# Soft-capped attention into a top-2 mixture of attention experts: the last two batches in packed passes of queries

## The chip, the cores and the metric

The kernel runs on one core of a Trainium2 chip. A core has five engines that run side by side and wait for each other through semaphores: TensorE (PE in the profile: matmuls and transposes into PSUM, with its weight loads as PEld), VectorE (DVE), ScalarE (ACT: tanh, exponentials, copies), GpSimd (POOL: casts, masks, the gate) and SyncE (SP: it issues DMA transfers). The metric is device microseconds of one execution. Three runs of the kernel before gave 313.25, 313.42 and 313.74 us, median 313.42.

## The reference

There are 8 batches, 12 heads, 448 positions and head size 64. The first stage is attention with a soft cap: scores are scaled by 1/8, passed through 30 tanh(s/30), and a softmax over the keys weighs v. The twelve heads of a position side by side are a row x of 768 numbers. The second stage is a mixture of four attention experts with a causal mask:

```python
scores = scale * np.matmul(q, k.transpose(0, 1, 3, 2))
scores = cap * np.tanh(scores / cap)
...
x = attn_out.transpose(0, 2, 1, 3).reshape(B, S, H * D)
logits = x @ w_gate
topk = np.argpartition(-logits, K, axis=-1)[..., :K]        # K = 2 of 4 experts
for e in range(E):
    q = x @ wq[e]; k = x @ wk[e]; v = x @ wv[e]
    scores = np.where(causal, -1000000000.0, scale * (q @ k.transpose(0, 2, 1)))
    a = softmax(scores)
    ye = a @ v @ wo[e]
    out += mask[..., None] * w[:, :, kk:kk + 1] * ye          # w: softmax over the two chosen logits
```

The softmax of either stage is made without its maximum: the exponentials are summed through a column of ones beside v, and the product is divided by that sum.

## The kernel before, in words

**First stage.** Two heads make a pair; there are 48 pairs, 6 a batch. A pair's q, k and v are loaded two pairs at a time (`load`), cast to 16 bits (`cast`, nearly all on POOL), and q and k are turned by TensorE and copied by VectorE into a tile `qk` (`tr`). Key rows are three chunks of 128 and a tail of 64. A step p then has three pieces: X (first key chunk of both heads, and the tails of both), Y1 and Y2 (second and third chunk). `fill` makes the scores into the PSUM tiles X (three banks) and Y (two banks), `tanh` runs on ScalarE over each piece, `expo` is one exponential over all seven rows of a step. `pv` multiplies with v, divides on VectorE (a reciprocal and a product) and `xt` turns the result into xT, from which the second stage of the batch reads. Three more PSUM banks, A0 to A2 (AUX), serve everything else.

**Steps.** In steps 0 to 41 (batches 0 to 6) a step is one pair with all its 448 queries. The pairs of batch 7 do their first 320 queries in steps 42 to 47; steps 48 and 49 do the last 128 queries of three pairs each. Thus there are 50 steps.

**Second stage.** For batches 0 to 5, `b_v`, `b_qk`, `b_gate` and `b_mask` project, choose and mask the queries by the chosen expert, and each of the two choices has one score block of 1024 columns (`b_score`) and its products (`b_pv`), sums (`b_ot`) and output (`b_wo`). For batch 6 (`FULL`), `e_score` and `e_pv` compute all four experts instead, in four blocks of 1024. Such a block takes the place of scores in X, and its exponential stands in ScalarE's list between those of the first stage. Batch 7's second stage (`last`, `last2`) runs after the first stage has ended: `last` for the first 320 queries, with a causal mask added in PSUM by a matmul (`negm`), and `last2` for the last 128.

**Order.** All instructions are recorded in a graph with costs (`Graph`, `Op`) and put in order by a list scheduler (`solve`) before they are issued. Each engine takes the most urgent ready instruction by its due time; the due times follow from ScalarE's fixed list of tanh and exponentials. `rank` adds a pseudo-random shift to the due time, drawn from `SEEDS`, one number for each 4 us of planned time. A `Group` holds one PSUM bank from its first matmul to its last reader. The order on each engine is fixed once built, and engines wait for one another at run time.

Of the kernel before, what the change touches and what calls it, by code (L numbers as in the profile page):

```python
# [8 lines left out]
f32 = mybir.dt.float32  # L9
# [13 lines left out]
SEEDS = (0, 0, 677, 116, 161, 0, 0, 56, 0, 513, 845, 569, 0, 188, 90, 308, 807, 654, 0, 873, 140, 943, 805, 400, 898, 250, 0, 621, 339, 0, 597, 460, 182, 0, 964, 592, 385, 0, 0, 0, 56, 980, 62, 160, 0, 0, 639, 563, 0, 0, 0, 105, 472, 832, 0, 567, 424, 0, 670, 583, 486, 783, 58, 224, 0, 0, 0, 0, 260, 212, 0, 946, 0, 0, 98, 0, 918, 79)  # L23
# [4 lines left out]
FDUE = 7.616  # L28
FULL = (6,)
XFULL = {5: (4, 5, 6, 7), 6: (4, 5, 6, 7)}  # L30
# [20 lines left out]
class Graph:  # L51
# [79 lines left out]
    def solve(self, when, banks, lent):  # L131
# [44 lines left out]
        while len(order) < n:  # L176
            best = None
            for e, rs in ready.items():
# [8 lines left out]
                def rank(x):  # L187
# [83 lines left out]
def kernel(  # L271
# [25 lines left out]
    PB = NP - HP  # L297
    W1 = 320
    NPV = NP + 2
    WIN1 = (0, 128, W1 - 128)  # L300
    TL = S - KM
    WIN = (0, 128, 256, S - 128)
    LB = B - 1

# [28 lines left out]
    PART = {"X": X[:, 0:2, :]}  # L333
# [66 lines left out]
    yp = [sb(f"yp{i}", [128, 7, S]) for i in range(NYP)]  # L400
    xk = [sb(f"xk{i}", [128, 4, 2, Dh]) for i in range(NXK)]
    rc2 = [sb(f"rc2_{i}", [128, 3, 2, 1], f32) for i in range(2)]
    xk2 = [sb(f"xk2_{i}", [128, 3, 2, Dh]) for i in range(2)]
    rca = [sb(f"rca{i}", [128, 2, 2, 1], f32) for i in range(4)]
# [3 lines left out]
    qB = [[sb(f"qB{i}_{r}", [128, S]) for r in range(2)] for i in range(2)]  # L408
    kB = [[sb(f"kB{i}_{r}", [128, S]) for r in range(2)] for i in range(2)]
# [6 lines left out]
    oT = [[sb(f"oT{i}_{r}", [128, S]) for r in range(2)] for i in range(2)]  # L416
# [12 lines left out]
    negm = sb("negm", [128, W1])  # L429
    neg2 = sb("neg2", [128, 2, 128])  # L430
    kL = sb("kL", [128, 2, 128])
    qL = sb("qL", [128, 2, 128])
    vL = sb("vL", [128, E, Dh + 1])
    p2 = yp[NPV % NYP].rearrange("p a s -> p (a s)")[:, 0 : E * 512].rearrange(
        "p (e c t) -> p e c t", e=E, c=4)
    oTL = [sb(f"oTL{i}", [128, 2, 128]) for i in range(2)]
    gt1 = [sb(f"gt1_{i}", sh, f32) for i, sh in enumerate(
        ([128, 3, E], [128, 3, E], [128, 3, E, E], [128, 2, 3, 1]))]
    gt2 = [sb(f"gt2_{i}", sh, f32) for i, sh in enumerate(
        ([128, 1, E], [128, 1, E], [128, 1, E, E], [128, 2, 1, 1]))]  # L440
# [89 lines left out]
    def setup_b():  # L530
# [25 lines left out]

        def lastc():
            nc.gpsimd.memset(vL[:, :, Dh : Dh + 1], 1.0)
            nc.gpsimd.memset(negm, 0.0)
            nc.gpsimd.memset(neg2, 0.0)  # L560
            nc.gpsimd.memset(neg2[64:128, 0, :], -30000.0)

        gp(0.9, lastc, w=["vL", "negm", "neg2"], due=150.0)

        def below(t, base):
            return lambda: nc.gpsimd.affine_select(
                out=t, in_=t, compare_op=ALU.is_ge, fill=-30000.0, base=base,
                pattern=[[1, 128]], channel_multiplier=-1)

        gp(0.4, below(negm[:, 0:128], 0), ["negm"], ["negm"], due=150.0)  # L570
        gp(0.4, below(negm[:, W1 - 128 : W1], -64), ["negm"], ["negm"], due=150.0)
        gp(0.4, below(neg2[:, 1, :], 0), ["neg2"], ["neg2"], due=150.0)
# [122 lines left out]
    def wid(p):  # L695
        return S if p < PB else W1 if p < NP else 3 * 128

    def of(p, what=None):


        if p < NP:
            return [p]
        ps = [PB + 3 * (p - NP) + i for i in range(3)]
        return ps if what is None else [ps[("X", "Y1", "Y2").index(what)]]

    def heads(p, what):
        dst = X if what == "X" else Y
        ci = {"X": 0, "Y1": 1, "Y2": 2}[what]
        t = qk[of(p, what)[0] % NQK]
        n = wid(p)  # L710
        for c in (ci,) if p < NP else range(KC):
            for g in range(2):
                r = slice(64 * g, 64 * (g + 1))
                o, qs = (slice(0, n), slice(0, n)) if p < NP else (
                    slice(128 * c, 128 * (c + 1)), slice(W1, S))
                nc.tensor.matmul(  # L716
                    dst[:, g, o], t[r, S + 128 * (c + 1) : S + 128 * (c + 2)], t[r, qs],
                    start=True, stop=True,
                )

    def tails(p):
        for i, m in enumerate(of(p)):
            t = qk[m % NQK]
            o, qs = (slice(0, wid(p)),) * 2 if p < NP else (
                slice(128 * i, 128 * (i + 1)), slice(W1, S))
            nc.tensor.matmul(X[:, 2, o], t[:, S : S + 128], t[:, qs], start=True, stop=True)  # L726

    def fill(p, what):
        def rd(p, what=None):
            return [y for m in of(p, what) for y in (  # L730
                ("qk", m % NQK, "k"), ("qk", m % NQK, "q"), ("qkw", m % NQK))]
# [26 lines left out]
    ACTS = {}  # L758
# [891 lines left out]
```

## Time and profile before

| | before |
|---|---|
| median of three runs | 313.42 us |
| span of the profiled execution | 311.6 us |
| the profiled execution's own time | not given; the median is 1.8 us above the span |
| busy: TensorE, VectorE | 284.4, 220.0 us |
| busy: ScalarE, GpSimd | 293.7, 176.3 us |
| read from and written to memory | 36.19, 11.01 MB |

The page's slices divide the span into 40 equal parts, with the busy share of an engine in tenths. The chain of waits follows what ended last back to what released it. In a timeline an idle time before an instruction stands in brackets with its releaser. A busy TensorE is not at its peak, since the ends of matmuls are modelled and overlap; starts are more reliable than durations.

### The profile page before, as it was taken

To read this page: it belongs to the slowest core of one execution; us is meant where nothing else is said; L and a number is where in the kernel's file an instruction comes from. 1 tells how busy PE (TensorE), PEld (TensorE's weight loads), DVE (VectorE), ACT (ScalarE), POOL (GpSimd) and SP (SyncE) were. 2 spreads that over 40 slices of the span, in tenths; PEclk is the share of its full clock that TensorE was granted. 3 is DMA by queue.
4 is the path that set the end of the run, shared out by engine and by line. 5 is a ranking of instruction groups with operands and counts; after the bars stand their busy time and mean duration, and the time that the engine had idled before them with its cause. 6 is when DMAs were issued, how large, how long until landed. Compare 5 with 4: busy or idle time off the path is not lost.

```text
span 311.6 us, 8990 instructions
## 1 busy us (share of the span) xinstructions
PE 284.4 (91%) x3508; PEld 189.8 (61%) x3508; DVE 220.0 (71%) x665; ACT 293.7 (94%) x250; POOL 176.3 (57%) x485
## 2 busy tenths in 40 slices
PE   7677879989899999999899989999999999998993
PEld 3344445567655766557665866668756675666761
DVE  3334655696777888597868877887868976686673
ACT  4799999999999999999999999999999999999673
POOL 7675345999836787377655593857685222332100
PEclk9978999999999999999999999999999999999999
DMA  6699999899998799167831896240000500032036
GB/s 187 151 225 233 256 290 244 210 280 240 238 260 198 217 252 226 45 207 198 235 67 64 235 238 170 58 163 21 0 2 2 178 2 4 0 114 67 2 136 221
DMA packets 65083, 47.79 MB, mean 153 GB/s; under 512 B 25744, under 2 KB 61328, under 8 KB 65040
## 3 DMA queue, kind: packets, MB, share of 16 engines
q1 hardware_dynamic: 64736, 46.98, 56.7%
q8 instruction: 27, 0.44, 0.6%
q10 hardware_dynamic: 304, 0.23, 0.2%
q14 instruction: 16, 0.13, 0.1%
HBM read 36.19 MB, written 11.01 MB: 151 GB/s over the span
## 4 chain that ended last, share of the span: by engine, by line
ACT 41%; PE 36%; DVE 7%; DMA 4%; SPq 4%; issue 4%; POOL 2%; DVEq 0%; ACTq 0%
ACT yp L768 22%; ACT yp L780 16%; PE A L802 4%; PE A L935 4%; PE Y L716 4%; PE A L910 3%; ACT pP L1070 3%; PE A L795 2%; DMA qf<-in_q_dram 2%; DVE ob L378 2%; PE X L1061 2%; DMA kf<-in_k_dram 2%; PE A L841 2%; PE A L1235 2%; PE A L662 2%
## 5 line engine op out<-in xcount | busy, mean ns | idle before, releaser
L780 ACT ACTIVATE yp<-yp 128x3136 f16<-128x3136 f16 (+4 forms) x51 | 140.4, 2757 | 0.0
L768 ACT ACTIVATE yp<-Y 128x896 f16<-128x896 f32 (+2 forms) x100 | 97.8, 978 | 3.1 <-PE Y L716 3.1
L768 ACT ACTIVATE yp<-X 128x1344 f16<-128x1344 f32 (+2 forms) x50 | 66.6, 1333 | 2.0 <-PE X L726 1.4
L802 PE MATMUL A<-v,yp 128*128 128x65 f16 x1116 | 55.3, 195 | 0.0
L802 PEld LDWEIGHTS <-yp 128*128 128x128 f16 x1116 | 48.9, 98 | 4.9 <-issue 3.1
L795 PE MATMUL A<-vtz,yp 128*128 128x130 f16 x186 | 41.5, 223 | 6.7 <-ACT yp L780 4.5
L826 DVE TENSOR_TENSOR xk<-A,rca 128x256 f16<-128x256 f32 (+1 forms) x96 | 39.7, 414 | 2.8
L716 PE MATMUL Y<-qk 64*128 64x448 f16 (+2 forms) x216 | 36.1, 341 | 2.5 <-ACT yp L768 1.6
L619 POOL CAST k<-kf 128x384 f16<-128x384 f32 x47 | 23.6, 510 | 20.2 <-PE A L662 10.8
L638 POOL CAST v<-vf 128x384 f16<-128x384 f32 x48 | 24.5, 512 | 17.1 <-PE A L802 15.2
L823 DVE RECIPROCAL rca<-A 128x4 f32<-128x4 f32 (+1 forms) x96 | 17.0, 177 | 21.0 <-PE A L802 20.4
L682 DVE COPY qk<-A 128x960 f16<-128x960 f16 x47 | 29.2, 649 | 3.1 <-PE A L652 2.8
L378 DVE COPY ob<-A 128x384 f32<-128x384 f32 (+1 forms) x54 | 29.0, 554 | 2.3 <-PE A L1235 0.9
L622 POOL CAST q<-qf 112x512 f16<-112x512 f32 x44 | 27.0, 617 | 4.8 <-DMA qf<-in_q_dram 4.2
L795 PEld LDWEIGHTS <-yp 128*128 128x128 f16 x186 | 18.1, 97 | 17.5 <-issue 8.3
L716 PEld LDWEIGHTS <-qk 64*128 64x128 f16 x324 | 14.0, 93 | 21.4 <-issue 16.1
L1235 PE MATMUL A<-wo,oT 128*128 128x384 f16 x112 | 25.4, 326 | 0.4
L850 DVE COPY xT<-A 128x448 f16<-128x448 f16 (+1 forms) x48 | 18.1, 378 | 9.7 <-PE A L841 9.4
L1193 DVE SCALAR_TENSOR_TENSOR oB<-A,rcb,mw 128x256 f16<-128x256 f32 x48 | 22.3, 480 | 1.6
L910 PE MATMUL A<-wvg,xT 128*128 128x260 f16 x168 | 22.1, 274 | 0.6 <-DVE xT L850 0.3
L662 PE MATMUL A<-ident,k 128*128 128x128 f16 x144 | 16.3, 224 | 5.3 <-POOL k L619 3.3
L1178 PE MATMUL A<-vB,pP 128*128 128x260 f16 x120 | 20.2, 275 | 0.9 <-DVE oB L1193 0.7
(250 smaller groups left out, 593.1 us busy)
## 6 DMA issues: line engine op xcount, KB each, us to landing
qf<-in_q_dram SPq DMA_DIRECT2D x23, 448.0 KB, 6.4
kf<-in_k_dram SPq DMA_DIRECT2D x23, 384.0 KB, 5.4
vf<-in_v_dram SPq DMA_DIRECT2D x23, 384.0 KB, 5.9
out_dram<-ob SPq DMA_DIRECT2D x23, 384.0 KB, 2.7
out_dram<-ob SPq DMA_DIRECT2D x9, 192.0 KB, 2.7
ktf<-in_k_dram SPq DMA_DIRECT2D x46, 32.0 KB, 5.1
vtf<-in_v_dram SPq DMA_DIRECT2D x46, 32.0 KB, 4.9
ob<-in_moe_wv_dram SPq DMA_DIRECT2D x2, 384.0 KB, 4.6
```

What stands on the lines that cost most here:

```text
L378: (nc.scalar.copy if o.eng == "ACT" else nc.vector.tensor_copy)(dst(), src())
L622: e(q16[i], qf[s][:, h].rearrange("p h (c d) -> p c h d", c=QC))
L638: nc.gpsimd.tensor_copy(v16[u][:, :, :, 0:Dh], vf[s][:, h].rearrange("p h (c d) -> p h c d", c=KC))
L682: lambda: nc.vector.tensor_copy(qk[t], bank16(g)[:, 0 : S + 512]),
L716: nc.tensor.matmul(dst[:, g, o], t[r, S + 128 * (c + 1) : S + 128 * (c + 2)], t[r, qs], start=True, stop=True,)
L768: ACTS[what, p] = act(c_act(n * (b - a)), lambda: nc.scalar.activation(y[:, a:b, 0:n], src[:, 0 : b - a, 0:n], AF.Tanh, scale=isc / capf), ...
L780: act(c_act(n * (b - a), False), lambda a=a, b=b, n=n: nc.scalar.activation(y[:, a:b, 0:n], y[:, a:b, 0:n], AF.Exp, scale=capf), ks, ks, f ...
L795: nc.tensor.matmul(ps[:, n, :, :], y[:, 2, w : w + 128], vtz[u], start=(n == 0), stop=False, skip_group_check=True,)
L802: nc.tensor.matmul(ps[:, n, h, :], y[:, SLOT[c][h], w : w + 128], v16[u][:, h, c, :], start=False, stop=(c == 2), skip_group_check=True,)
L826: dve(c_dve(128 * m), lambda g=g, i=i, rc=rc, m=m: nc.vector.tensor_tensor(xk[p % NXK][:, 2 * i : 2 * i + m, :, :], view(g)[:, 0:m, :, 0:D ...
L910: nc.tensor.matmul(bank(g)[:, 0 : E * Dh + E], xT[x][:, j, w : w + 128], wvg[:, j, :], start=(j == 0), stop=(j == NDC - 1),)
L1235: nc.tensor.matmul(bank(g)[:, 0 : D // 2], oT[x][r][:, w : w + 128], wo2[r][:, c0:c1], start=(r == 0), stop=(r == 1),)
```

## The change

1. The last two batches are cut by queries into passes (`PARTS`): batch 6 into 0 to 256 and 256 to 448, batch 7 into 0 to 256, 256 to 384 and 384 to 448. A step of these passes holds several pairs side by side: two of 256 columns, two of 192, three of 128, or six of 64 (`ST`). Steps 0 to 35 are as before. Steps 36 to 47 replace steps 36 to 49, and a pair's loads and transposes come when it is first needed (`FIRST`), two pairs a step.
2. Batch 6's second stage is made by pass with four experts (`p_qk`, `p_v`, a gate for each pass, `p_score`, `p_pv`): its score blocks are smaller (`PIECES`: 768 or 512 columns, instead of four of 1024), placed at steps 42, 45 and 46, on Y or X. k and q of a pass share a bank and are copied together into one tile (`kqB`).
3. Batch 7's first pass has its projections, values and gate during the first stage; its scores come after it (`LATE`, `late`), then products and output (`p_pv`). Its passes of 128 and 64 queries run in `tail` (`ENDING = 2`), which replaces `last` and `last2`. The masks there are made by POOL (`masks`) on the exponentials, not by a matmul.
4. Batch 5's two score blocks both come at step 40 (`XLAST`), one on Y, one on X; before they came at steps 41 and 42.
5. The tiles v16 and vtz have 12 buffers instead of 8, qk has 12 instead of 6; yp is 512 wide instead of 448.
6. All queues get a new order: other `SEEDS`, and a table `SHIFT` with one byte for each instruction, which moves its due time by up to 12 us.

```diff
+SHIFT = bytes.fromhex(
...
-FDUE = 7.616
-FULL = (6,)
-XFULL = {5: (4, 5, 6, 7), 6: (4, 5, 6, 7)}
+DV = (3.0, 1.4)
+DQ = (2.0, 1.0)
+DW = (12.261, 1.8)
+PARTS = {6: ((0, 256), (256, 448)), 7: ((0, 256), (256, 384), (384, 448))}
+SEQ = ((6, 0), (6, 1), (7, 0), (7, 1), (7, 2))
+XOFF = (5, 6)
+XLAST = (4, 4)
+PIECES = {42: ((6, 0, 0), (6, 0, 1)), 45: ((6, 1, 0), (6, 1, 1)), 46: ((6, 1, 2), (6, 1, 3))}
+LATE = ((7, 0, 0), (7, 0, 1))
+ENDING = 2
...
                         d += ((u.idx * 40503 + k * 9973) % 1009 / 1009.0 - 0.5) * JIT
+                    d += (SHIFT[u.idx] - 128) / 10.0
...
+    ST = [((p,), 0, S) for p in range(HP * SEQ[0][0])]
+    ENDS = {}
+    for b_, i_ in SEQ:
+        q0, q1 = PARTS[b_][i_]
+        m = min(512 // (q1 - q0), 3 if q1 - q0 > 64 else HP)
+        ps = list(range(HP * b_, HP * (b_ + 1)))
+        ST += [(tuple(ps[i : i + m]), q0, q1) for i in range(0, HP, m)]
+        ENDS[len(ST)] = (b_, i_)
+    NPV = len(ST)
...
-    NST, NQ16, NKZ, NV, NQK, NYP, NXK = 4, 3, 6, 8, 6, 4, 4
+    NST, NQ16, NKZ, NV, NQK, NYP, NXK = 4, 3, 6, 12, 12, 4, 4
...
+    def p_qk(b, i, ref):
+        x = b % 2
+        q0, q1 = PARTS[b][i]
+        n = q1 - q0
+        for r in range(2):
+            g = Group(AUX, 2.4)
+            for j in range(NDC):
+                for z in range(2):
+                    pe(n, lambda g=g, r=r, j=j, z=z: nc.tensor.matmul(
+                        bank(g)[:, n * z : n * (z + 1)], (wk2, wq2)[z][r][:, j, :],
+                        xT[x][:, j, q0:q1], start=(j == 0 and z == 0), stop=(j == NDC - 1),
+                        skip_group_check=True),
...
+    def late(b, i, pc):
...
+        pe(0, mm, [("kqB", x, r, z) for z in range(i + 1)], [k0, k1], gs[0],
+           occ=sum(c_pe(y[3]) for y in part), name=f"sL{r}{h}")
...
+        for e in range(2):
+            ee = 2 * r + e
+            act(c_act(n), lambda e=e, ee=ee: nc.scalar.activation(
+                pB[ee][:, base + o0 : base + o0 + n], bank(gs[e])[:, 0:n], AF.Exp, scale=isc),
...
+    def masks(r, c, o, ks, q):
...
+        def fn():
+            blk = pP[r][lo:128, :, o : o + n]
+            nc.gpsimd.affine_select(
+                out=blk, in_=blk, compare_op=ALU.is_ge, fill=0.0, base=0,
+                pattern=[[0, 2], [1, n]], channel_multiplier=-1)
...
-        for x in (0,) if p == 0 else (p + 1,) if p < NP - 1 else ():
+        for x in (0,) if p == 0 else [m for m in range(NP) if FIRST[m] == p + 1]:
...
+                jobs = [(b_score, y) for y in exps.get(p, ())]
+                jobs += [(p_score, y) for y in PIECES.get(p, ())]
+                for t, (fn, y) in enumerate(jobs):
+                    fn(*y, "X" if t == len(jobs) - 1 else "Y")
...
+                if ENDS.get(p, SEQ[-1]) not in SEQ[-ENDING:]:
+                    bb, i = ENDS[p]
+                    p_qk(bb, i, ref)
+                    p_v(bb, i, ref)
+                    ns = chunks(bb, i)
+                    for fn in (b_gate, b_gate1, b_gexp, b_gate2):
+                        fn(bb, ns[0], ns[-1] + 1, i)
...
     expo(NPV - 1, (("X", "Y1"), ("Y2",)))
     pv(NPV - 1)
-    apart("left", (b_score.last, 0.9), [("X0",), ("X1",)])
-    apart("right", (ACTS["Y2", NPV - 1], 0.8), [("Y0",), ("Y1",)])
-    last(fixed_last())
+    for t in range(2):
+        xt(NPV - 1, sub=t)
+    for y in LATE:
+        late(*y)
+    for bb, i in SEQ[:-ENDING]:
+        if any(y[:2] == (bb, i) for y in LATE):
+            p_pv(bb, i, fixed_last())
+    for y in SEQ[-ENDING:]:
+        tail(*y, fixed_last())
```

More of the change, by code (lines that the diff above doesn't have):

```diff
@@ L693, in tr_first_tails, with wid, rel @@
             [("tps", p, "t")], [("qk", t, "t")], gt)
[L695 to L706, printed above, removed]
+    def wid(k):
+        ps, q0, q1 = ST[k]
+        return len(ps) * (q1 - q0)
+    def rel(k):
+        w = ST[k][2] - ST[k][1]
+        return WIN if w == S else (0,) if w < 128 else tuple(range(0, w - 127, 128)) + ((w - 128,) if w % 128 else ())
@@ L707, in heads, with entries @@
+    def entries(k):
+        ps, q0, q1 = ST[k]
+        return [(m, i * (q1 - q0) + o) for i, m in enumerate(ps) for o in rel(k)]
+    def heads(k, what):
         dst = X if what == "X" else Y
[L708 to L711, printed above, removed]
+        c = {"X": 0, "Y1": 1, "Y2": 2}[what]
+        ps, q0, q1 = ST[k]
+        for i, m in enumerate(ps):
+            t, o = qk[m % NQK], (q1 - q0) * i
@@ L1200, in b_ot @@
         x = b % 2
-        so = oB[0] if b in FULL else oS
-        for i in range(0 if b in FULL else 2):
+        so = oS
+        for i in range(2):
             n = slice(2 * i, 2 * i + 2)
@@ new lines, in pieces @@
+    def pieces(b, i):
+        q0, q1 = PARTS[b][i]
+        blocks, o = [], 0
+        for c in range(4):
+            s = max(q0, CH[c])
+            if s < q1:
+                blocks.append((c, o, s, q1 - s))
+                o += q1 - s
+        base = 64 if q1 == S else 704
+        half = [y for y in blocks if y[1] + y[3] <= 512]
+        if len(half) == len(blocks):
+            return base, [blocks]
+        half = [y for y in blocks if y[1] + y[3] <= 384]
+        return base, [half, blocks[len(half) :]]
```

904 lines of the change are left out of this document (467 added, 437 removed).

## The prediction

> **What bounds the kernel now.** I read the page from the top: span, busy shares, slices, then the chain of waits.
>
> ```profile
> span 311.6 us, 8990 instructions
> PE 284.4 (91%) x3508; PEld 189.8 (61%) x3508; DVE 220.0 (71%) x665; ACT 293.7 (94%) x250; POOL 176.3 (57%) x485
> PE   7677879989899999999899989999999999998993
> ACT  4799999999999999999999999999999999999673
> PEclk9978999999999999999999999999999999999999
> ACT 41%; PE 36%; DVE 7%; DMA 4%; SPq 4%; issue 4%; POOL 2%; DVEq 0%; ACTq 0%
> ```
>
> ScalarE is full from the second slice to the thirty-seventh, and the last three slices have another limit. The view of stages splits the span at the instant at which the last exponential of the first stage ends (290.68 us, from its row below):
>
> ```profile
> core 0: us, PE busy (x) PEld busy (x) DVE busy (x) ACT busy (x) POOL busy (x), PEclk, DMA share, GB/s
> 0.00:30.67 30.67, 22.71 (x212) 12.49 (x213) 12.04 (x35) 23.28 (x20) 21.06 (x100) 0.90 0.84 199
> 240.00:290.68 50.68, 47.90 (x668) 33.21 (x664) 38.77 (x126) 50.54 (x47) 14.84 (x39) 1.00 0.16 57
> 290.68:311.60 20.92, 15.95 (x188) 10.72 (x186) 12.96 (x49) 11.00 (x28) 0.00 (x0) 1.00 0.37 133
> ```
>
> So there are three parts: a start in which ScalarE idles for 7.4 of 30.67 us; a body in which it idles for 0.14 of 50.68 us; and an ending of 20.92 us, in which TensorE is busiest (15.95) and ScalarE half empty. An edit is worth what it does to ScalarE's list in the body, to ScalarE's idle time in the start, and to the longest path in the ending.
>
> The execution shown has a span of 311.6 us; its own total isn't given, so what lies around it I take from the median of the runs, 313.42 - 311.6 = 1.8 us, and carry over unchanged. All terms are differences against this execution.
>
> **Part 1, the ScalarE list of the body.** The chain gives the pace of ScalarE, in starts (three tanh of a step together, then its exponential, then a second-stage exponential):
>
> ```profile
> 79.74 0.92 ACT pP L1070
> 86.15 2.80 ACT yp L768 x3
> 88.95 2.70 ACT yp L780
> 258.75 2.05 ACT yp L768 x3
> 260.80 1.96 ACT yp L780
> 281.79 2.43 ACT yp L768 x3
> 284.22 2.33 ACT yp L780
> ```
>
> These are a step of 448 queries (5.50 us), of 320 (4.01) and of 384 (4.76). Per query column of seven tiles the two lines give (2.80 - 2.05)/896 = 0.84 ns and (2.70 - 1.96)/896 = 0.83 ns an element, with 0.17 us fixed for the three tanh and 0.08 for the exponential. A packed step of 512 columns then costs (2.80 + 0.375) + (2.70 + 0.37) = 6.25 us (estimate by those lines). Before: 42 x 5.50 + 6 x 4.01 + 2 x 4.76 + 16 x 0.92 = 279.3. After: 36 x 5.50 + 6 x 6.25 + 6 x 4.76 + 12 x 0.92 + four exponentials of 768 elements at 0.71 + two of 512 at 0.49 = 278.9. The same elements pass, in eight instructions fewer: -0.4 us.
>
> The Trainium skill (ScalarE: Activation LUTs, section What ACT_TABLE_LOAD costs) states 0.833 ns an element and 186 ns fixed, of which 93 ns overlap with the next instruction. The slope agrees with the 0.84 above; the fixed part doesn't quite, 0.06 to 0.08 by the rows against 0.09. By the page the eight instructions would be worth 0.74 us instead of 0.4; I keep the rows.
>
> **Part 2, the start.** The order of all queues is solved anew with other seeds and the new table SHIFT, so instructions that the diff doesn't name move too.
>
> ```profile
> 6.24 0.92 ACT L768 ACTIVATE yp<-Y 128x896 f16<-128x896 f32 x1 [0.91 <-PE Y L716]
> 8.56 1.29 ACT L768 ACTIVATE yp<-X 128x1344 f16<-128x1344 f32 x1 [1.41 <-PE X L726]
> 11.40 0.92 ACT L768 ACTIVATE yp<-Y 128x896 f16<-128x896 f32 x1 [1.55 <-PE Y L716]
> 14.19 2.83 ACT L780 ACTIVATE yp<-yp 128x3136 f16<-128x3136 f16 x1
> 8.29 0.66 DVE L682 COPY qk<-A 128x960 f16<-128x960 f16 x1 [0.19 <-PE A L652]
> 10.72 0.34 PE L662 MATMUL A<-ident,k 128*128 128x128 f16 x3 [1.53 <-POOL k L619]
> ```
>
> The wait of 1.55 us at 11.40 isn't for data. Pair 1 had been transposed and copied by 8.95 us; the scores stood in TensorE's queue behind the transposes of pair 2, which waited for POOL's cast of k until 10.72. In the built order of the changed kernel those scores stand ahead of pair 2. Against that, pair 1's k is issued on SP sixth instead of third (three places later at about 0.55 us, some 1.6 us), and POOL casts it behind more memsets, because v16 and vtz have 12 buffers instead of 8. I put that cast at 8.3 to 8.8 us instead of 6.1, the copy's end near 10.2, and the third tanh near 10.5: -0.9 us. The near bound is the whole wait with what it cost behind it (-1.3); the far one is that POOL's longer list makes pair 2 late (k cast near 13.9, needed near 15.5), +0.6.
>
> **Part 3, the body from step 36 on.** Batches 6 and 7 go in passes; 14 steps (six of 448, six of 320 and two of 384 columns) become 12, and pairs 36 to 41 and 42 to 47 are each needed within three steps. By the built order, with a matmul at its column count over the 2.3 columns a ns of the rows of part 4, TensorE issues about 5.0 to 5.8 us a step there against 5.1 to 6.9 us on ScalarE; the tightest is step 38, 5.8 against 5.9. Batch 5's second stage moves one step earlier, its two score blocks side by side on X and Y at step 40; batch 6's is split into two passes with their own gates on POOL; batch 7's first pass (24 matmuls of 256 columns, 12 of 260) moves from the ending into the body. Transposes are spread: the keys of pairs 0 to 39 stand ahead of the tail scores of step 34, those of pair 47 ahead of step 42's, for use in step 44, which the 12 instead of 6 buffers of qk allow. New waits that I expect: scores behind a POOL cast or behind a held auxiliary bank. The nearest row is TensorE's wait for POOL's cast of k:
>
> ```profile
> PE A L662 <- POOL k L619: 3.3, 4, 1.5
> ```
>
> Its mean is 0.8 us, its longest 1.5. I take one of mean length, +0.8; bounds 0 less the 0.6 us of idle left in the body (part of it before 240 us), and +3.0 for two of the longest. SP's stores of batch 3 stand behind the last loads in the new order; they wait for nothing that ScalarE needs soon, since the output buffers are wanted six steps later: nothing.
>
> **Part 4, the ending.** Before, all of batch 7's second stage (448 queries) and the last steps of batch 6's come after the last exponential. After, it holds scores, products and output of the first 256 queries of batch 7 and the whole second stage of the other 192, beside what is left of batch 6.
>
> ```profile
> 288.05 2.63 ACT L780 ACTIVATE yp<-yp 128x1920 f16<-128x1920 f16 x2
> 306.60 0.82 PE L1294 MATMUL A<-wo,oTL 128*128 128x384 f16 x4 [0.53 <-ACT oTL L378]
> 307.51 0.48 ACT L378 COPY ob<-A 128x384 f32<-128x384 f32 x1 [0.96 <-PE A L1294]
> 308.02 0.35 ACTq L1303 DMA_DIRECT2D out_dram<-ob  x1
> 290.23 0.18 PE Y0s L872 x6
> 291.55 0.56 PE A L1461 x10
> 292.16 0.33 PE X0s L1347 x3
> 298.95 0.76 PE A L1235 x4
> ```
>
> The exponential ends at 288.05 + 2.63 = 290.68, the last matmul at 307.4, the last copy at 307.99: 17.3 us; stores to the end take 3.6 more and stay. TensorE after: 72 matmuls of 65 columns at 0.03, 5 of 130 at 0.06, 26 of 128 at 0.056, 38 of 64 or fewer at 0.03, 12 of 256 at 0.11, 20 of 384 at 0.19: 10.2 us, against 16.8 elapsed before. So TensorE no longer sets the end. VectorE does:
>
> ```profile
> 284.44 0.17 DVE L1440 COPY gt<-A 128x12 f32<-128x12 f32 x1 [0.92 <-PE A L1326]
> 287.07 0.18 DVE L1453 RECIPROCAL gt<-gt 128x3 f32<-128x3 f32 x1
> 287.75 0.56 DVE L883 TENSOR_TENSOR xk<-X2s,rc 128x384 f16<-128x384 f32 x1
> 303.68 0.56 DVE L378 COPY ob<-X0s 128x384 f32<-128x384 f32 x1
> 304.82 0.42 DVE L1272 TENSOR_TENSOR oB<-Y0s,slL 128x256 f16<-128x256 f32 x1
> ```
>
> By the built order 50 VectorE instructions follow the last step's products, as many as the 49 of before (12.96 us): 34 small ones at 0.17 (5.8), two of 384 columns and four output copies at 0.56 (3.4), six of 256 columns and the 512-column copy at 0.42 (2.9), three small copies at 0.25 (0.8): 12.9 us, and 0.9 until the first can start: 13.8 us instead of 17.3, -3.5. The masks that were matmuls become selects on POOL; POOL has nothing else there (0 us busy in the stage), and the four that follow the last exponentials lie beside VectorE's list. The bounds: TensorE's 10.2 with the 1.5 us of waiting it has now and the copy, 12.3 (-5.0); and every small instruction at 0.25, the pace of the dependent gate chain (12 of them and one 0.48 copy from 284.44 to 287.25), 16.5 (-0.8).
>
> **The sum.** 313.42 - 0.4 - 0.9 + 0.8 - 3.5 = 309.4 us. All terms at their good ends give 313.4 - 0.4 - 1.3 - 0.6 - 5.0 = 306.1.
>
> **The rivals.** One: TensorE's clock falls in the ending. The clock is 7 and 8 tenths in the third and fourth slice, where TensorE is 7 tenths busy. The new ending has 10.2 us of matmul in 13.8, less than the 15.95 in 20.92 now, with holes while VectorE works. For: those slices. Against: the last slice, 3 tenths busy, still shows 9. If the clock halved in the second half, some 5 us of matmul would take 5 more, half of it beside VectorE: 311.9 us. The Trainium skill (TensorE: Matmul & The Clock Gate, section What's actually happening) has this as its rule: after an idle window of about 3.4 us the clock halves; the ending has no such hole, so by the page as well this is unlikely.
>
> Two, the other sign: packed steps starve ScalarE. Pairs arrive two a step in steps 36 to 38 and 42 to 44; if POOL's casts or the three auxiliary banks hold the scores up by 1.0 us in each of six steps, the body pays 6.0 instead of 0.8: 314.6 us. It decides from 0.8 us a step on, where 4.8 us eat the gain. For: one wait of 1.5 us is seen, and VectorE is 38.77 of 50.68 us busy before the work grows denser. Against: TensorE's counts leave room, and the transposes are ahead.
>
> Three: the change doesn't do what it says: the late pass of batch 7 and two tails follow one another in queue order and the ending is as long as before, 312.7 to 313.4 us.
>
> **How the numbers follow.** The forecast, 306.1 to 311.2 us, has 0.58; the clock or an ending at its far bound (311.2 to 312.6) 0.20; the third rival 0.06; starved steps 0.16. A measurement of this kernel tells about 0.2% (0.6 us) from no change, so faster ends at 312.8: 0.58 + 0.20 and a part of the third make 0.80, same 0.04, slower 0.16. The range goes from 306.0 to 313.8 and leaves about one in ten out on each side.
>
> **What would show it.** Right: the last exponential of the first stage ends near 290.2 us, the last copy 13 to 14.5 us later, VectorE over 85% busy in between; the third tanh starts near 10.5 us. Wrong: waits of ScalarE for scores of more than 2 us in all between steps 36 and 47, with POOL casts or VectorE copies as releasers; a granted clock below 0.9 in the ending; or an ending above 16 us.

## The result and the profile after

The changed kernel takes 308.48 us (median of four runs, 308.27 to 311.66) against 313.34 us (312.83 to 313.74) for the kernel before beside it: a ratio of 0.9871, 95% interval 0.9825 to 0.9918. Forecast were 309.4 us and 306.0 to 313.8. The four executions of the changed kernel spread by over 3 us, the four of the kernel before by 0.9 us; experiment 7 shows one place where such a spread arises. The profiled execution is one of 308.59 us. Medians in this document are of all executions, while the ratios leave out those more than 1.5% above the fastest of their kernel, which are one each in e2, e3 and e12 (medians without it 308.78, 307.37 and 308.99 us) and one of the kernel before beside e8, e9 and e10.

The page after (span, busy shares, slices):

```profile
span 306.9 us, 9228 instructions
PE 286.0 (93%) x3626; PEld 196.2 (64%) x3626; DVE 219.8 (72%) x667; ACT 290.9 (95%) x239; POOL 187.2 (61%) x538
PE   7787989999999998999999999999999999999994
ACT  4999999999999998999999999999999999999953
PEclk9988799999999999999999999999999999999998
```

ScalarE is full from the second slice to the 38th of 40 (before from the third to the 37th), and one slice in the middle (the sixteenth, near 121 us) is an 8 where all were 9. The view of stages, cut where the last exponential of the first stage ends (288.89 us) and where the last copy ends (302.87 us):

```profile
0.00:30.67 30.67, 23.04 (x208) 12.41 (x209) 11.44 (x34) 25.67 (x22) 21.37 (x109) 0.91 0.88 208
240.00:288.89 48.89, 48.01 (x709) 36.16 (x707) 38.70 (x118) 48.88 (x41) 17.94 (x61) 1.00 0.21 75
...
288.89:302.87 13.98, 13.26 (x197) 9.30 (x196) 11.23 (x54) 8.53 (x24) 4.85 (x16) 1.00 0.24 81
```

The columns are those of the prediction's view of stages: length, then busy time of TensorE, its weight loads, VectorE, ScalarE, POOL, then granted clock. In the start ScalarE is busy 25.67 us instead of 23.28. In the packed steps it is busy 48.88 of 48.89 us. In the ending TensorE is busy 13.26 of 13.98 us (95%) and VectorE 11.23 (80%), at a full clock.

ScalarE's timeline, the rows that answer to those of the prediction, with every wait between the first and the last exponential:

```profile
8.34 1.29 ACT L819 ACTIVATE yp<-X 128x1344 f16<-128x1344 f32 x1 [1.09 <-PE X L776]
9.68 0.92 ACT L819 ACTIVATE yp<-Y 128x896 f16<-128x896 f32 x1
12.50 2.82 ACT L831 ACTIVATE yp<-yp 128x3136 f16<-128x3136 f16 x1
34.39 0.92 ACT L819 ACTIVATE yp<-Y 128x896 f16<-128x896 f32 x1 [0.51 <-PE Y L767]
121.65 0.92 ACT L819 ACTIVATE yp<-Y 128x896 f16<-128x896 f32 x1 [0.90 <-PE Y L767]
286.33 2.56 ACT L831 ACTIVATE yp<-yp 128x1920 f16<-128x1920 f16 x2
```

The difference of the two profiled executions falls apart into four pieces without a rest:

| piece | before | after | difference |
|---|---|---|---|
| start to the first exponential | 14.19 | 12.50 | -1.69 |
| first exponential to the end of the last (body) | 276.49 | 276.39 | -0.10 |
| end of the last exponential to end of the last copy (ending) | 17.31 | 13.98 | -3.33 |
| last copy to the end of the span (stores) | 3.61 | 4.03 | +0.42 |
| span | 311.6 | 306.9 | -4.7 |

In the body ScalarE waits 1.11 us before (at 30.67 and 74.94) and 1.41 us after; without the waits it takes 275.38 and 274.98 us, -0.40.

In the chain of waits the ending is TensorE's, with one stretch that is nearly all VectorE's (295.4 to 297.4 us) and the last copy:

```profile
292.24 0.50 PE A L1454 x8
294.30 0.54 PE A L1473 x4
296.25 0.38 DVE oB L1415
297.00 0.39 DVE oB L1415
297.44 0.40 PE X1s L1424 x4
...
299.40 0.43 PE A L1202 x2
300.76 0.43 PE X0s L1552 x2
301.19 1.10 PE A L1552 x6
302.32 0.55 DVE ob L454
```

That is another engine than the one the prediction named.

### The profile page after: what moved, and what is told of

The parts are those of the page before. It is cut to its first block, busy times and chain, and to the rows that moved or that the text cites. A ratio compares the mean times of both kernels' runs of the same rounds, so it can differ in the third digit from the quotient of the medians.

```text
span 306.9 us, 9228 instructions
## 1 busy us (share of the span) xinstructions
PE 286.0 (93%) x3626; PEld 196.2 (64%) x3626; DVE 219.8 (72%) x667; ACT 290.9 (95%) x239; POOL 187.2 (61%) x538
## 4 chain that ended last, share of the span: by engine, by line
ACT 53%; PE 32%; DVE 5%; issue 5%; POOL 4%; POOLq 0%; DVEq 0%; ACTq 0%
ACT yp L819 27%; ACT yp L831 21%; PE A L954 4%; PE A L860 4%; PE Y L767 3%; ACT pP L1094 3%; PE A L929 2%; PE A L1202 2%; DVE ob L454 2%; PE A L854 2%; ACT pP L1316 1%; PE X L1085 1%; PE A L901 1%; PE X L767 1%; PE A L712 1%
## 5 line engine op out<-in xcount | busy, mean ns | idle before, releaser
L831 ACT ACTIVATE yp<-yp 128x3136 f16<-128x3136 f16 (+4 forms) x49 | 138.6, 2832 | 0.0
L819 ACT ACTIVATE yp<-Y 128x896 f16<-128x896 f32 (+2 forms) x96 | 94.3, 982 | 2.4 <-PE Y L767 2.3
L819 ACT ACTIVATE yp<-X 128x1344 f16<-128x1344 f32 (+2 forms) x48 | 65.1, 1356 | 1.2 <-PE X L776 1.1
L860 PE MATMUL A<-v,yp 128*128 128x65 f16 (+1 forms) x1116 | 57.2, 196 | 0.0
L860 PEld LDWEIGHTS <-yp 128*128 128x128 f16 (+1 forms) x1152 | 51.8, 100 | 4.0 <-issue 1.6
L854 PE MATMUL A<-vtz,yp 128*128 128x130 f16 (+1 forms) x186 | 41.9, 225 | 2.9 <-ACT yp L831 1.6
L767 PE MATMUL Y<-qk 64*128 64x448 f16 (+4 forms) x264 | 35.5, 309 | 2.6 <-ACT yp L819 2.2
L854 PEld LDWEIGHTS <-yp 128*128 128x128 f16 (+1 forms) x192 | 19.0, 99 | 14.1 <-issue 7.7
L916 DVE COPY xT<-A 128x448 f16<-128x448 f16 (+3 forms) x46 | 17.7, 385 | 7.8 <-PE A L901 7.5
L962 DVE CAST kqB<-A 128x448 f16<-128x448 f32 x24 | 14.9, 622 | 10.2 <-PE A L954 10.2
L702 PE MATMUL A<-ident,q 112*128 112x112 f16 x192 | 21.7, 216 | 0.0
```

Source lines behind the costliest of these rows:

```text
L767: nc.tensor.matmul(dst[:, g, o : o + q1 - q0], t[r, S + 128 * (c + 1) : S + 128 * (c + 2)], t[r, q0:q1], start=True, stop=True,)
L819: ACTS[what, p] = act(c_act(n * (b - a)), lambda: nc.scalar.activation(y[:, a:b, 0:n], src[:, 0 : b - a, 0:n], AF.Tanh, scale=isc / capf), ...
L831: act(c_act(n * (b - a), False), lambda a=a, b=b, n=n: nc.scalar.activation(y[:, a:b, 0:n], y[:, a:b, 0:n], AF.Exp, scale=capf), ks, ks, f ...
L854: nc.tensor.matmul(view(g)[:, n], y[:, 2, w : w + rw], vtz[u], start=(n == 0), stop=False, skip_group_check=True,)
L860: nc.tensor.matmul(view(g)[:, n, h, :], y[:, SLOT[c][h], w : w + rw], v16[u][:, h, c, :], start=False, stop=(c == 2), skip_group_check=True,)
```

## The experiments

All stages below are read as in the table above, in each kernel's profiled execution; times are medians beside the kernel before on the same chip.

| run | first exponential | waits in the body | ending | stores | time | before | ratio of the two, 95% |
|---|---|---|---|---|---|---|---|
| e1_start_order | 12.76 | 2.15 | 17.32 | 3.69 | 312.94 | 313.28 | 0.9955 to 1.001 |
| e8_start_order2 | 12.77 | 1.23 | 17.31 | 3.68 | 312.80 | 312.98 | 0.9965 to 1.0033 |
| e4_no_gates | 12.55 | 1.26 | 13.95 | 4.42 | 309.11 | 313.28 | 0.9818 to 0.9927 |
| e5_half_output | 12.66 | 4.66 | 13.16 | 4.57 | 309.59 | 313.09 | 0.9838 to 0.9941 |
| e2_logits_together | 12.66 | 2.00 | 12.99 | 4.03 | 308.78 | 313.28 | 0.9792 to 0.987 |
| e3_logits_wide | 12.54 | 0.66 | 12.84 | 3.98 | 307.70 | 313.28 | 0.9793 to 0.9926 |
| e6_before_plain | 14.55 | 3.74 | 18.32 | 4.41 | 319.18 | 313.09 | 1.0167 to 1.0215 |
| e7_after_plain | 14.14 | 9.59 | 15.88 | 4.54 | 321.98 | 313.09 | 1.0252 to 1.0301 |
| e9_after_late_plain | 12.41 | 7.26 | 15.88 | 4.65 | 316.92 | 312.98 | 1.0107 to 1.0197 |
| e10_before_late_plain | 14.91 | 0.44 | 18.33 | 4.63 | 315.03 | 312.98 | 1.0035 to 1.0087 |
| e11_after_again | 12.57 | 2.96 | 13.97 | 4.05 | 308.84 | 313.01 | 0.983 to 0.9919 |
| e12_logits_together5 | 12.79 | 2.18 | 12.99 | 3.98 | 309.37 | 313.01 | 0.9814 to 0.9901 |

### 1. Which engine sets the ending: VectorE without its gates, TensorE without half of its output

The gates of the last two passes are VectorE's small instructions; half of batch 7's output product is TensorE's alone.

```diff
+            for y in gt1:                        # weights set ahead
+                nc.gpsimd.memset(y[0], 0.25)
+                nc.gpsimd.memset(y[3], 1.0)
...
-            dve(c, fn, ...                       # gate_tail
+            dve(c, lambda: None, ...
-        act(0.1, lambda: nc.scalar.activation(z, z, AF.Exp), ...
+        act(0.1, lambda: None, ...
```

> The changed kernel without the gates of the last two passes (their 24 small VectorE instructions and two small exponentials are left out, the weights of the experts are set to 0.25 ahead; TensorE does all it did). As predicted (VectorE sets the ending with 12.9 us of work): some 24 x 0.13 = 3.1 us less work on it, last copy about 11 us after the last exponential instead of 13.98. TensorE theory (it carries the path from 288.6 to 295.4 and from 297.4 on): only the 2 us between can shrink, last copy at 12.8 to 13.7 us.

The same stage of this kernel, cut at its last copy:

```profile
288.93:302.88 13.95, 13.19 (x198) 9.30 (x196) 9.56 (x32) 8.32 (x23) 4.91 (x16) 1.00 0.24 80
```

VectorE has 22 instructions fewer in the stage and is busy 9.56 us instead of 11.23; the ending is 13.95 us instead of 13.98. Even TensorE's theory had expected a little more (12.8 to 13.7): the VectorE stretch of the chain is reciprocals and products of the late pass, not gates.

```diff
-                for r in range(2):              # normed, and likewise b_wo for batch 7
-                    nc.tensor.matmul(..., oTL[n % 2][:, r, 0:rw], wo2[r][:, c], start=(r == 0), stop=(r == 1))
+                nc.tensor.matmul(..., oTL[n % 2][:, 0, 0:rw], wo2[0][:, c], start=True, stop=True)
```

> The changed kernel without the second half (two of four experts) of the output product of batch 7: 10 of its 20 matmuls of 384 columns are left out, all in the ending; every copy and store stays. TensorE theory: the path runs through about six of the ten pairs, 0.16 us each less, last copy 0.7 to 1.2 us earlier than 13.98 after the last exponential. As predicted (VectorE): within 0.3 us of 13.98.

The ending is 13.16 us, 0.82 less, with VectorE's instructions all there. (The matmuls left out are 8 of 16, not 10 of 20 as the expectation says; at 0.16 us they are 1.3 us.) So the gates taken from VectorE are worth nothing in the ending (0.03 us for 1.67 us of busy time), and work taken from TensorE is worth more than half of its length. VectorE isn't far behind: in e5 the last three output copies stand back to back on it (1.50 us from 304.23 us), so there it sets the last stretch. And VectorE's reciprocals and products on the chain, some 2 us, were left in by both runs. That the medians of these two runs lie above the changed kernel's comes from elsewhere: stores of 4.42 and 4.57 us instead of 4.03, and in the second a body of 279.91 us (experiment 7).

### 2. What TensorE spends there: matmuls of two widths in turn

In the last pass each pair of key and query matmuls (128 columns of weights) is followed by one for the gate's logits whose weights are 64 columns wide (`tail`, L1460). TensorE's timeline of the changed kernel, first and last of the six:

```profile
292.52 0.19 PE L1454 MATMUL A<-xT,wk 128*128 128x64 f16 x1
292.55 0.19 PE L1454 MATMUL A<-xT,wq 128*128 128x64 f16 x1
292.67 0.19 PE L1460 MATMUL A<-wvg,xT 128*64 128x4 f16 x1
292.80 0.20 PE L1454 MATMUL A<-xT,wk 128*128 128x64 f16 x1
...
294.10 0.19 PE L1460 MATMUL A<-wvg,xT 128*64 128x4 f16 x1
294.23 0.61 PE L1473 MATMUL A<-wvg,xT 128*128 128x256 f16 x4
```

From start to start a key matmul takes 0.03 us; the step to the 64-wide weights takes 0.12, and the step back 0.13. The 18 matmuls take 1.71 us (292.52 to 294.23).

```diff
-                    if r == 0:
+                    for jj in () if r else (j,) if rw == 128 else range(NDC) if j == NDC - 1 else ():
...
-                                xT[x][:, j, max(WIN[c], q0) : WIN[c] + 128], wvg[:, j, E * Dh :],
+                                xT[x][:, jj, max(WIN[c], q0) : WIN[c] + 128], wvg[:, jj, E * Dh :],
...
```

> The changed kernel, with the six gate-logit matmuls of the last pass (64-column weights, 4 columns) issued together behind its six pairs of key and query matmuls instead of one after each pair. Theory T1 (a change of the weights' width between two matmuls costs about 0.11 us each way, 12 such changes on the path): that group of 18 matmuls takes about 0.7 us instead of 1.7, and the last copy ends 0.8 to 1.1 us earlier after the last exponential: about 12.9 to 13.2 instead of 13.98. Theory T2 (VectorE sets the ending's length, as predicted): the group is shorter but the last copy comes within 0.3 us of 13.98. Theory T3 (the matmuls of this group wait for something else, data or a bank): the group still takes 1.5 us or more.

```profile
293.71 0.19 PE L1454 MATMUL A<-xT,wk 128*128 128x64 f16 x1
...
294.15 0.35 PE L1460 MATMUL A<-wvg,xT 128*64 128x4 f16 x6
294.43 0.61 PE L1473 MATMUL A<-wvg,xT 128*128 128x256 f16 x4
```

With one change there and one back the group takes 0.72 us, and the ending 12.99 us, 0.99 less. All of the saving arrives at the last copy.

Is it the change of width, or that the matmuls alternate at all? The next run keeps the alternation and makes the weights 128 wide:

```diff
-                                bank(g)[0:rw, 2 * n + E * t : 2 * n + E * (t + 1)],
-                                xT[x][:, j, max(WIN[c], q0) : WIN[c] + 128], wvg[:, j, E * Dh :],
+                                bank(g)[:, 2 * n + E * t : 2 * n + E * (t + 1)],
+                                xT[x][:, j, WIN[c] : WIN[c] + 128], wvg[:, j, E * Dh :],
```

> The changed kernel, with the order kept as it is, but the last pass's logit matmuls given 128 columns of weights (queries 320 to 447) instead of 64; the gates of the last 64 queries of batch 7 are then those of other queries. T1 (width change): the group of 18 matmuls takes about 0.6 us instead of 1.7, and the ending 12.9 to 13.3 us. If it is the alternation itself, or a wait for data, that costs: 1.5 us or more as now, ending 13.7 to 14.2. T2 (VectorE): group shorter, ending within 0.3 us of 13.98.

The group then takes 0.51 us (291.80 to 292.31) and the ending 12.84 us. So it is the width, at about 0.1 us for each change: (1.71 - 0.51)/12. The Trainium skill (TensorEngine Tiling (Array Packing), section Key Properties) says that a change of the tiling mode drains TensorE. The trace agrees in that each change costs time, some 0.1 us here; whether it is a drain, it doesn't show. `solve` does price such a change, `SWITCH = 0.1`, but only between the 64-row score matmuls and the others (`o.half`); the 64-column logits count there as ordinary matmuls.

### 3. The same again, beside the changed kernel, with more rounds

> The changed kernel unchanged, beside the next run on the same chip, as the base for it: 308.0 to 309.0 us, ratio to before 0.985 to 0.988, ending near 13.98 us.

> The changed kernel with the last pass's six gate-logit matmuls issued together (as in e2_logits_together), more rounds, beside the changed kernel on the same chip. Theory T1 (width changes on the path): 0.8 to 1.1 us less than the changed kernel by the medians, ending near 13.0 us. If the ending's gain is lost again in the stores or in the body: medians within 0.4 us.

The endings are again 13.97 and 12.99 us, but the medians are 308.84 and 309.37 us, with intervals to before that overlap. The expected 0.8 to 1.1 us by the medians did not come. The best two executions of each are 307.44 and 307.51 us against 307.06 and 307.15. So the shorter ending is shown by the stage in three kernels (0.99, 1.14 and 0.98 us in e2, e3 and e12), and a shorter time of the whole kernel isn't: the executions of either kernel spread by over 4 us, more than the gain.

### 4. The start: a wait that is only queue order, and what becomes of the gain

```diff
     order = G.solve(when, AUX, XB + YB)
+    k2 = next(o for o in order if o.name == "trk2")
+    order.remove(k2)
+    order.insert(1 + next(i for i, o in enumerate(order) if o.name == "sT_1"), k2)
```

> The kernel before, with one instruction group moved: the transposes of pair 2's keys stand behind the scores of pair 1 and their tail, not ahead of them. Queue-order theory (the 1.55 us wait at the third tanh was only TensorE's queue): the third tanh starts near 9.9 us instead of 11.40, the first exponential near 12.7 instead of 14.19, and the whole kernel is 1.3 to 1.5 us faster, about 311.9. Rival (the scores would have waited anyway, for pair 1's copy or for a score bank; the changed start is owed to the other moves on POOL and SP): third tanh within 0.4 us of 11.40 and the time within 0.5 us of before.

The third tanh starts at 9.92 us instead of 11.40 and the first exponential at 12.76 instead of 14.19: the wait was only order, as predicted. But the median falls by 0.3 us, not 1.4, and the interval reaches from 1.4 us faster to 0.3 us slower; in the profiled execution the span is 311.5 us against 311.6. ScalarE's rows of this run, and TensorE's before them:

```profile
12.76 2.82 ACT L780 ACTIVATE yp<-yp 128x3136 f16<-128x3136 f16 x1
...
22.11 0.92 ACT L768 ACTIVATE yp<-Y 128x896 f16<-128x896 f32 x1 [1.03 <-PE Y L716]
...
25.06 0.92 ACT L768 ACTIVATE yp<-Y 128x896 f16<-128x896 f32 x1 [0.86 <-PE Y L716]
```

```profile
20.36 0.50 PE L662 MATMUL A<-ident,k 128*128 128x128 f16 x3 [2.29 <-POOL k L619]
```

ScalarE runs ahead by 1.43 us and meets pair 4, whose keys are cast when they were cast before. The next run moves pair 4's transposes too:

```diff
+    k4 = next(o for o in order if o.name == "trk4")
+    order.remove(k4)
+    order.insert(1 + next(i for i, o in enumerate(order) if o.name == "sY2X_2"), k4)
```

> The kernel before with the move of the run e1_start_order and one more: the transposes of pair 4's keys stand behind the scores of step 2's second keys and step 3's first, not ahead of them. In e1_start_order the gain of 1.43 us at the first exponential was given back at 22.11 and 25.06 us (waits of 1.03 and 0.86), where TensorE had stood 2.29 us at the transposes of pair 4 for POOL's cast of k. Queue-order theory: the same fault one step later; the waits of ScalarE at 22 and 25 us fall below 0.3 each and the kernel is 1.2 us or more faster than before (312.1 or less). Pace-of-the-loads theory: pairs 3 and 4 arrive when they do, ScalarE waits for them a step later (1 us or more in all between 20 and 35 us), and the time stays within 0.6 us of before.

```profile
23.28 0.92 ACT L768 ACTIVATE yp<-Y 128x896 f16<-128x896 f32 x1 [0.20 <-PE Y L716]
...
29.69 0.92 ACT L768 ACTIVATE yp<-Y 128x896 f16<-128x896 f32 x1 [0.81 <-PE Y L716]
```

```profile
27.52 0.95 POOL L619 CAST k<-kf 128x384 f16<-128x384 f32 x2 [2.23 <-DMA kf<-in_k_dram]
```

The waits at 22 and 25 us go, one of 0.81 comes at 29.69, and behind it POOL waits 2.23 us for a load of k. The time is 312.80 against 312.98 us. So by the medians little is left of what the order gave in the kernel before. But the one profiled execution kept 1.0 us of it (span 310.6): its waits in the body are only 0.12 us longer than before, and the interval (0.9965 to 1.0033) doesn't exclude such a gain. That the loads take the rest back is shown by waits in e1, not in e8. In the changed kernel the 1.69 us of the start are not taken back by such waits in the profiled execution (0.51 us at 34.39). Its loads run denser early on, by the two windows of 10 to 20 us (the last two columns are the DMA share and GB/s; the first row is before, the second after):

```profile
10.00:20.00 10.00, 6.58 (x63) 3.14 (x64) 3.20 (x8) 8.60 (x8) 7.42 (x37) 0.90 0.75 192
```

```profile
10.00:20.00 10.00, 7.83 (x76) 4.52 (x75) 3.63 (x9) 10.00 (x8) 8.38 (x40) 0.83 1.04 261
```

That these denser loads keep the gain is argued from the rows; no run isolates it.

### 5. Structure or order: both kernels without their tuned order

```diff
-SEEDS = (...)
+SEEDS = ()
-                    d += (SHIFT[u.idx] - 128) / 10.0      # in the changed kernel
```

> The kernel before, its order solved without the seeds (no shifts at all). If the tuned order matters little, within 0.5 us of 313.3; if it carries much, 3 us or more slower. To be read beside the next run: the difference of the two is what the packed steps and passes are worth with neither order tuned.

> The changed kernel, its order solved without seeds and without the table. Theory S (structure: the gain is in the passes and packed steps): faster than the untuned kernel before by 3.3 us or more, most of it in the ending (14 to 15 us instead of 17.3 or so). Theory O (order: the table keeps the packed steps fed and the start short): slower than the changed kernel by 4 us or more, with ScalarE waiting over 2 us in the packed steps (from 240 us on) and the untuned pair within 1.5 us of each other.

Untuned, the changed kernel takes 321.98 us and the kernel before 319.18. So without a searched order the change makes the kernel 2.8 us slower: the ending is 2.4 us shorter (15.88 against 18.32), but ScalarE waits 9.59 us in the body instead of 3.74. Of these waits 4.48 us lie past 240 us (1.13 in the kernel before), and 5.11 us ahead of it (2.61), in steps that the change leaves as they are but for order and buffers. Theory S falls. Theory O had the waits right, but not that the untuned pair lie within 1.5 us. Each kernel was untuned in one way only, so 2.8 us holds for these two orders. The tuned order is worth 6.1 us to the kernel before (against 313.09) and 13.1 to 13.5 us to the changed one (against 308.84 and 308.48).

### 6. Where the order is worth it: late or early

```diff
-                    k = SEEDS[int(t0 / 4.0)] if t0 < 4.0 * len(SEEDS) else 0
+                    k = SEEDS[int(t0 / 4.0)] if t0 < 200.0 else 0
-                    d += (SHIFT[u.idx] - 128) / 10.0                    # e9 alone
+                    d += (SHIFT[u.idx] - 128) / 10.0 * (t0 < 200.0)     # e9 alone
```

> The changed kernel with seeds and table acting only in the first 200 us of the planner's time, so that the start and some 33 steps are the changed kernel's and the packed steps and the ending are in the untuned order. Theory O (the packed steps starve ScalarE unless their order is searched): from 240 us to the last exponential ScalarE waits 3 us or more, and the kernel is 5 to 9 us slower than the changed one, at 313 to 317. Theory E (the table's worth of 13.5 us lies early, in the many steps before): within 2.5 us of the changed one, ending 15 to 16 us.

ScalarE's rows at step 40 of this run, and then those of the changed kernel:

```profile
246.89 1.02 ACT L1094 ACTIVATE pP<-Y 128x1024 f16<-128x1024 f32 x1 [3.88 <-PE Y L1085]
248.82 1.02 ACT L1094 ACTIVATE pP<-X 128x1024 f16<-128x1024 f32 x1 [0.91 <-POOL pP L1111]
```

```profile
241.99 1.15 ACT L1094 ACTIVATE pP<-Y 128x1024 f16<-128x1024 f32 x1
242.89 1.16 ACT L1094 ACTIVATE pP<-X 128x1024 f16<-128x1024 f32 x1
```

In the untuned late order ScalarE waits 4.8 us in one place: batch 5's two score blocks, which the change puts side by side on Y and X a step earlier. TensorE isn't idle then; it is busy 6.62 of the 6.89 us from 240 us to that row, with batch 6's projections (L1268) and the transposes of batch 5's masked queries (L1056) ahead of the scores. In the changed kernel neither block waits. With its late order untuned the changed kernel takes 316.92 us, 8.4 us more than tuned: 4.8 in this place, 1.9 in the ending, 0.6 in the stores, and 1.6 of a longer wait near 122 us, which isn't the late order's (experiment 7), less 0.5 of the wait at 34.39, which is gone in this execution.

> The kernel before with its seeds acting only in the first 200 us of the planner's time. Its last steps hold one pair each, so by theory O its untuned late order costs little: within 2 us of before, ScalarE waiting under 1.5 us from 240 us on. If it loses as much as the changed kernel's late part does (5 us or more), the packing isn't what makes the order matter.

The kernel before, late order untuned, takes 315.03 us, 2.05 more; ScalarE waits 0.44 us in its whole body, and the loss is in the ending (+1.02 us) and the stores (+1.02), while a first exponential 0.72 us later and a body 0.76 us shorter cancel. So it is the packed late part that needs its order searched, and in one step above all. An untuned early order alone wasn't tried; the waits of e7 ahead of 240 us say that it has a price too.

### 7. The spread: a hole that the new order makes near 116 us

Of two profiled executions of the same kernel (the changed one, and e11), the second lost 1.7 us more in the body, 1.1 of it near this place (waits of 0.19 and 1.81 us against 0.90). POOL's and TensorE's rows of e11 at that place:

```profile
114.62 0.51 POOL L688 CAST v<-vf 128x384 f16<-128x384 f32 x1 [2.13 <-DMA vf<-in_v_dram]
...
116.09 0.52 POOL L1104 TENSOR_SCALAR_AFFINE_SELECT pP<-pP 128x384 f16<-128x384 f16 x1
```

```profile
116.67 0.39 PE L1144 MATMUL A<-vB,pP 128*128 128x260 f16 x1 [1.36 <-POOL pP L1104]
```

```profile
116.00:118.00 2.00, 1.33 (x11) 0.95 (x12) 0.80 (x5) 2.00 (x2) 1.87 (x6) 0.68 1.02 200
118.00:120.00 2.00, 2.00 (x12) 0.72 (x11) 1.43 (x5) 1.81 (x2) 2.00 (x6) 0.50 0.31 77
```

The mask of a second-stage block stands on POOL behind a cast of v whose load hasn't landed, and casts of k and q; the products of that block stand on TensorE behind the mask, and scores behind them. TensorE idles 1.36 us, and in this execution the granted clock then falls to 0.68 and 0.50; ScalarE waits 1.81 us at 123.40. In the changed kernel's profiled execution TensorE idles 1.23 us at the same place, the clock stays at 1.00 and ScalarE waits 0.90:

```profile
116.00:118.00 2.00, 1.68 (x18) 0.95 (x18) 1.56 (x7) 2.00 (x2) 1.92 (x5) 1.00 0.84 181
118.00:120.00 2.00, 2.00 (x24) 1.43 (x21) 1.93 (x7) 2.00 (x3) 1.88 (x5) 1.00 0.27 47
```

Over the eight profiled executions that hold this part of the order (the changed kernel's, e2, e3, e4, e5, e9, e11, e12) the longest wait there is 0.66 to 2.49 us, and the clock divides them. In five (e2, e5, e9, e11, e12) it falls to 0.50 for 2 to 3 us soon after the hole, and ScalarE's wait is 1.72 to 2.49 us; in three (the changed kernel's, e3, e4) it stays at 1.00, and the wait is 0.66 to 1.01. The length of the hole doesn't decide it alone: 1.25 to 1.74 us in the five, 0.99 to 1.34 in the three. The kernel before and the changed kernel without its searched order (e7) have no wait of ScalarE near there, and their clock is 1.00 from 112 to 124 us, so the hole belongs to the searched order. The slowest executions were not profiled, so how much of the whole spread comes from here stays open. A version with that cast moved behind the mask wasn't tried.

## Why the prediction was right, and where its steps were not

**Part 1, ScalarE's list: -0.4.** Measured -0.40 (body without waits). The step held. (Six instructions fewer pass in the body, not eight: two steps of four go, and two more score blocks come. The -0.4 is added up from the durations and doesn't use the count; the 0.74 us set beside it does, and is a third too high.)

**Part 2, the start: -0.9.** Measured -1.69, outside the near bound of -1.3. That the wait was queue order is shown by e1. The step that failed is "the copy's end near 10.2, and the third tanh near 10.5": it put pair 1's copy ahead of the third tanh. That tanh is pair 0's Y2 and needs only pair 0's scores, and these stand ahead of pair 1's in TensorE's queue. The rows of the changed kernel, TensorE's and VectorE's:

```profile
9.28 0.36 PE L767 MATMUL Y<-qk 64*128 64x448 f16 x2
9.82 0.36 PE L767 MATMUL X<-qk 64*128 64x448 f16 x2 [0.18 <-DVE qk L732]
```

```profile
9.10 0.66 DVE L732 COPY qk<-A 128x960 f16<-128x960 f16 x1 [1.22 <-PE A L702]
```

Only the scores into X, for the fourth tanh, waited for the copy (its end 9.76, where 10.2 was forecast); the third tanh started at 9.68, right behind the second. Besides, what such a gain is worth at the end depends on the loads behind it, which the prediction named only for pair 2: with the start moved, the kernel before meets pair 4 first (e1).

**Part 3, the body: +0.8 for a new wait in the packed steps.** Measured +0.30 (waits of 1.41 against 1.11 us), inside the bounds. But the place was wrong: from 240 us on ScalarE waits 0.01 us. The new wait lies near 121 us, where the diff changes nothing but the order and the number of buffers; its kind was right (behind a POOL cast), its size inside the bounds by luck. That the transposes are ahead of the packed steps held; the place that is really short is batch 5's two blocks at step 40, which the prediction mentioned and did not price. The searched order covers it, and the unsearched late order doesn't (e9).

**Part 4, the ending: -3.5.** Measured -3.33, 13.98 us against 13.8 forecast. The attribution failed: "TensorE no longer sets the end. VectorE does." TensorE's 10.2 us came out as 13.26 busy, 95% of the stage: the sum has 173 matmuls where the stage has 197, and some 1.2 us are changes of weight width; VectorE's 12.9 us came out as 11.23, 80% (over 85% was forecast). Without the gates nothing moves, without half the output product 0.82 us do. Two sums of similar size stood side by side, and the larger was taken for the path without asking in which order the work comes. That -3.5 fits is luck: VectorE's 13.8 us lay close to what TensorE's path took. The prediction also compared 10.2 us in 13.8 with 15.95 in 20.92, where the 20.92 holds 3.61 us of stores without a matmul; up to the last copy TensorE was busy 15.95 of 17.31 us (92%) before. So TensorE nearly filled the ending before and after, and 2.69 of the 3.33 us gained are its busy time falling from 15.95 to 13.26. (The far bound's 0.25 us for a dependent small instruction is high too: the rows from 284.44 to 287.25 hold 11 of them and the 0.48 copy, 0.21 each.)

**Stores: they stay.** Measured +0.42: the last store is issued in 0.47 us instead of 0.35, and the stores before it are bunched closer. In the other kernels the same piece is 3.7 to 4.7 us (3.61 before); what sets it stays open.

**The rivals.** The clock rival fell in the ending (1.00 until the last copy). The Trainium skill's rule (TensorE: Matmul & The Clock Gate, section What's actually happening: a fall after an idle window of some 3.4 us) fits there. Near 116 us the measurement differs from it: single holes of 1.25 to 1.74 us came ahead of a granted 0.50 in five executions, so here the fall came after holes well short of that length. The starvation rival is not what happened, but without the searched order it is: 4.8 us in one step with the late order untuned (e9), 4.5 past 240 us with all of it untuned, and then 2.8 us slower than the untuned kernel before (e7). It was given 0.16 and would have been near the truth for the change without seeds and table; its form, 1.0 us in each of six steps, was wrong. The third rival fell.

The sum came out 0.9 us too high by the medians (309.4 against 308.48): the start gave 0.8 more than forecast, the body's waits took 0.5 less, the ending gave 0.2 less and the stores took 0.4, 0.7 us in all, so errors of both signs met; the remaining 0.2 us is how the profiled executions stand to the medians.

## What to carry to other kernels

Where two engines' sums are within a few us of each other, find the path from the chain and the order of the work, and check it by taking work from each in turn; the two sums alone don't tell. A packed or denser schedule may be slower until the order of its tightest step is searched: price that step, not the mean. Keep matmuls of equal weight width together, and look for masks queued behind a cast whose load is late.

## What the runs showed of the hardware

A change between weights of 128 and of 64 columns costs TensorE about 0.1 us each way, though the matmuls themselves are 0.03 us apart: 12 changes make 18 matmuls take 1.71 instead of 0.51 us. A single hole of 1.25 to 1.74 us in a busy stretch of TensorE was followed by a granted clock of 0.50 for 2 to 3 us in five executions, and holes of 0.99 to 1.34 us by none in three. ScalarE's wait behind it was 1.72 to 2.49 us in the five and 0.66 to 1.01 us in the three, so one such hole can part two executions of nearly the same code by 1 us and more. What decides between the two isn't shown.
